# Attention and two feed-forward blocks on one core: a planner that weighs the array's tile form, other ranks, and the opening scores in pieces

## The chip, the core and the metric

One core of a Trainium2 chip. The metric is the device time of one execution in microseconds (us), the median of three runs. Engines: PE is TensorE (matmuls), with PEld for its weight loads, DVE is VectorE, ACT is ScalarE, POOL is GpSimd, SP is the queue that issues all DMAs here. Between engines there are only semaphores, and each engine works off its instructions in the order in which the program was written.

## The reference

Shortened; the inputs are q, k, v of 4 batches, 8 heads, 576 rows and 64 columns, and all sizes are in float32.

```python
# attention: causal window of 128, ALiBi slopes
scores = q @ k.T / 8 + slopes[h] * -abs(i - j)
scores = where((i - j >= 0) & (i - j < 128), scores, -1e9)
attn = exp(scores - max); attn = attn / (sum(attn) + 1e-9)
x = (attn @ v)                     # as 2304 rows of 512
# first block: 512 -> 1024 -> 512
h = x @ w_in
solu = h * softmax(h)
x = (layernorm(solu) * g_ln) @ w_out
# second block: 512 -> 1536 -> 512
out = (silu(x @ w_gate) * (x @ w_val)) @ w_out2
```

## The kernel before

Weights and activations are split into a high and a low fp32r part, so a product of two matrices is three matmuls (lines 605, 938 and 1100). The work runs in three stages that overlap.

**Attention** has 20 steps c (4 batches of 5 steps; the fifth, t = 4, has 64 rows instead of 128) with four pairs of heads each. For each half of a step (two pairs) PE does the *scores* (lines 405 and 412); for each pair DVE, ACT and one of three engines do the softmax (lines 440 to 463), PE transposes the result (line 481), and DVE and ACT copy it to `pt`, once masked (line 488, "late") and once whole (line 491). For each half PE then multiplies with the *values* (line 520): `v` of the step before, and `vd`, the difference of this step's `v` and the last one's.

**First block**: 18 token tiles i. `up(i)` is four pieces of six matmuls of 512 columns (x times w_in, line 605). ACT, DVE and POOL make the solu and the norm, `flip(i)` is eight PE transposes (line 687), and `down1(g)`, for two token tiles, is eight pieces of twelve matmuls of 256 columns (line 605, `lnT` times `wout`).

**Second block**: 36 sets of seven products (line 938). In a set some banks are copied out and written again: s1, s5 and u2 are ACT's copies (lines 954, 959, 961), g1, g2 and v2 are DVE's additions (956, 964, 967), m1 its multiplication (972). The last product, over 252 groups, is line 1100.

All weights come in as 64-bit words and are unpacked ("decode", lines 258 to 266 on ACT, DVE and POOL, then 220 and 224 or 226). Tile `dw` holds what was fetched; `DEC1 = (3, 2)` gives it three buffers while attention runs.

**Tile forms.** Three kinds of matmul use the array in parts: scores with 64 rows by 32 columns (line 412), the scores of a batch's first step with 64 by 128 (line 405), values with 128 by 64, or 64 by 64 for the late products of a short step. Everything else but the transposes of a short step (64 by 128) uses the whole array, 128 by 128.

**The order** is made while the program is written. `Emitter` holds a list of operations that are ready, with a modelled time, and takes, on the engine that is free first, the one with the lowest rank. A rank comes from its task: the step's place for attention (`rank_of`), `i + LEAD` for token tiles, `set_rank` for sets. The modelled cost of a PE operation knows nothing of tile forms.

Of the kernel before, what the change touches and what calls it, by code (L numbers as in the profile page):

```python
# [34 lines left out]
DEC1 = (3, 2)  # L35
# [9 lines left out]
PAIRED = 0  # L45
VDB = 2
PW_2 = -0.5
LEAD = 3.2
R_FLIP = 1.0
R_DOWN = 4.0  # L50
PW_IN = [-0.6, -0.3, -0.29, -0.28, 0.07, 0.08, 0.09, 0.1]
PW_OUT = 4.4
B_DVE = 1600.0
B_ACT = 700.0
HALVES = [(0, 1), (1, 0), (0, 0)]
HB = NC2 // 2


BIAS = {"DVE": B_DVE, "ACT": B_ACT}

# [20 lines left out]

class Emitter:
# [6 lines left out]
    def __init__(self):  # L89
        self.busy, self.pending, self.count, self.open = {}, [], 0, {}  # L90
        self.now = 0.0

# [52 lines left out]
    def _submit(self, at, rank, engine, cost, fn, deps=(), extra=0.0):  # L145
        return self._queue(at, rank, [(engine, cost, fn)], deps, extra)

    def _queue(self, at, rank, ways, deps=(), extra=0.0):
# [3 lines left out]
        op = [rank, self._tick(), at, ways, extra, ev]  # L152
# [12 lines left out]
        return ev  # L165
# [5 lines left out]
    def run(self):  # L171
        while self.pending:
# [7 lines left out]
            t, _, _, op, (engine, cost, fn, *_) = min((x for x in ops if x[0] <= first), key=lambda x: x[1:3])  # L180
# [10 lines left out]
def attention_then_two_ffns(ctx: ExitStack, tc: tile.TileContext, qk, v, w_in, w_out, g_ln, w2, ident_d, base_d, tri_d, out):  # L191
# [58 lines left out]
    def unpack(d, words, got):  # L250

        lw, hw = words[:, :, 0], words[:, :, 1]
        hf = hw.bitcast(F32)
        yield got
        a = lw.bitcast(I32)
        r = yield (ACT, t_act(512), lambda: nc.scalar.activation(a, lw, AF.Copy, scale=2.0 ** -29))  # L258
# [3 lines left out]
        x = yield (ACT, t_act(512), lambda: nc.scalar.activation(bf, hf, AF.Abs, scale=2.0 ** -112))  # L262
        x = yield (DVEP, t_dve(512, True), lambda: nc.vector.tensor_scalar(b, b, 3, None, ALU.logical_shift_left), [x])  # L263
        x = yield (DVEP, t_dve(512), lambda: nc.vector.scalar_tensor_tensor(  # L264
            b, hw, 0x80000000, b, ALU.bitwise_and, ALU.bitwise_or), [x])
        x = yield (POOL, t_pool(512), lambda: nc.gpsimd.tensor_tensor(  # L266
            b.bitcast(I32), b.bitcast(I32), a, ALU.add), [x, r])
        em.give(d["dw"], x)
        return bf, x, d["db"]

    def decode(hi, lo, src, scale=None, even=False):
# [5 lines left out]
        x = yield (high(hi, bf, 512), [x])  # L277
        ways = low(lo, bf, hi, 512)
        x = yield (fair(ways) if even else ways, [x])
# [100 lines left out]
    def score(c, qd):  # L380
# [19 lines left out]
        def scores():  # L400
            for j in range(2):
                if t == 0:
                    for r in range(2):
                        rows = slice(r * D, (r + 1) * D)
                        nc.tensor.matmul(banks[ks[r]][:, j * 256:j * 256 + P], raw[c][rows, 2 * qd + j],  # L405
                                         kt[rows, 2 * qd + j, 0:P], start=True, stop=True)
                    continue
                for i in range(0, n, Q):
                    o, k0 = j * 256 + i, (t - 1) * P + i
                    for r in range(2):  # L410
                        rows = slice(r * D, (r + 1) * D)
                        nc.tensor.matmul(banks[ks[r]][i:i + Q, o:o + P + Q], raw[c][rows, 2 * qd + j, i:i + Q],
                                         kt[rows, 2 * qd + j, k0:k0 + P + Q], start=True, stop=True)

        x = yield (PE, 450 if t == 0 else 450 if t == 4 else 700, scores)
# [9 lines left out]
    def attend(u):  # L425
# [12 lines left out]
        if t:  # L438
# [3 lines left out]
                halves[0:n, :, P:P + n]), [d] + tri_ok)  # L442
        ex, ds, x = [], [], d
        for j in range(2):
            d = yield (DVE, t_dve(P), lambda j=j: nc.vector.tensor_tensor_reduce(  # L445
                e[0:n, j], sc[0:n, j * 256:j * 256 + P], bias[0:n, 2 * pr + j, bs],
                -0.125, 3.0e38, ALU.add, ALU.min, st[0:n, j:j + 1]), [x])
            ds.append(d)
        for j, d in enumerate(ds):
            ex.append((yield (ACT, 93 + t_act(P, True, True), lambda j=j: nc.scalar.activation(  # L450
                e[0:n, j], e[0:n, j], AF.Exp, bias=st[0:n, j:j + 1], scale=-1.0,
                accum_out=sc[0:n, j:j + 1]), [d, ds[0]])))
# [5 lines left out]
        def normalize(eng):  # L458
# [6 lines left out]
        x = yield (DVE, 360, invert, ex)  # L465
# [3 lines left out]
                    (POOL, t_pool(2 * P), lambda: normalize(nc.gpsimd))], [x])  # L469
# [13 lines left out]
        x = yield (PE, 218, flip_p, ident_ok)  # L483
# [3 lines left out]
        if t:  # L487
            ys.append((yield (DVE, t_dve(w), lambda: nc.vector.tensor_tensor(  # L488
                pt[0:n, 1, :, 0:n], tp[0:n, :, 0:n], tri[0:n, 1, 0:n].unsqueeze(1).to_broadcast([n, 2, n]), ALU.mult),
                [x])))  # L490
        ys.append((yield ([(ACT, t_act(w, False), lambda: nc.scalar.copy(pt[:, 0, :, 0:n], tp[:, :, 0:n])),  # L491
                           (DVE, t_dve(w), lambda: nc.vector.tensor_copy(pt[:, 0, :, 0:n], tp[:, :, 0:n]))], [x])))
# [4 lines left out]
        units = (pr - 1, pr) if c >= PAIRED else (pr,)  # L497
        if len(units) == 2 and pr % 2 == 0:
            halved[u].settle(max(y.time for y in ys))
            return  # L500
        if pr < len(units):
            yield px_s
            px_of[c] = yield bank_s
        else:
            yield started[u - len(units)]
        if len(units) == 2:
            yield halved[u - 1]
# [5 lines left out]
        def values():  # L513
            for r in units:
                for late in (1, 0) if t else (0,):
                    kp = n if late else P
                    for j in range(2):
                        h = 2 * r + j
                        src = vd[c] if late else vt[c - 1] if t else vt[c]
                        nc.tensor.matmul(px[j * 64:(j + 1) * 64, r, 0:n], src[0:kp, h * 64:(h + 1) * 64],  # L520
                                         pts[c * NPAIR + r][0:kp, late, j, 0:n], start=(late == 1 or t == 0), stop=(late == 0),
                                         skip_group_check=True)

        x = yield (PE, 100 + 450 * len(units), values, [loaded[c]])
# [15 lines left out]
        while done < n:  # L540
# [7 lines left out]
            y = yield (high(hi, src, 4 * w, False), [x])  # L548
            y = yield (low(lo, src, hi, 4 * w, False), [y])
# [121 lines left out]
    def flip(i):  # L671
# [9 lines left out]
        for q in range(2):  # L681
# [8 lines left out]
            x = yield (PE, 436, turn)  # L690
            y = yield (high(hi, tp, 512, False), [x])
            y = yield (low(lo, tp, hi, 512, False), [y])
# [230 lines left out]
    def products(s):  # L923
# [30 lines left out]
        s1 = yield (ACT, t_act(NH, False), lambda: nc.scalar.copy(t[:, 0], sd), [x1])  # L954
        x6 = yield product(kd, "s2", [x1, s1])
        g1 = yield (DVE, t_dve(NH), lambda: nc.vector.tensor_add(t[:, 0], t[:, 0], sx), [x2, s1])  # L956
        em.give(bank_s, g1, kx)
        g1 = yield (ACT, t_act(NH), lambda: nc.scalar.activation(t[:, 0], t[:, 0], AF.Silu), [g1])  # L958
        s5 = yield (ACT, t_act(NH, False), lambda: nc.scalar.copy(t[:, 2], sb), [x5])  # L959
        x3 = yield product(kb, "s4", [x5, s5])  # L960
        u2 = yield (ACT, t_act(NH, False), lambda: nc.scalar.copy(t[:, 1], sd), [x6])  # L961
        yield y_ok[p][3]
        x7 = yield product(kd, "s3", [x6, u2])
        g2 = yield (DVE, t_dve(NH), lambda: nc.vector.tensor_add(t[:, 1], t[:, 1], sb), [x3, u2])  # L964
        em.give(bank_s, g2, kb)
        g2 = yield (ACT, t_act(NH), lambda: nc.scalar.activation(t[:, 1], t[:, 1], AF.Silu), [g2])
        v2 = yield (DVE, t_dve(NH), lambda: nc.vector.tensor_add(t[:, 2], t[:, 2], sd), [x7, s5])  # L967
# [4 lines left out]
        m1_ = yield (DVE, t_dve(NH), lambda: nc.vector.tensor_mul(t[:, 0], t[:, 0], sd), [x4, g1])  # L972
# [240 lines left out]
```

## Time and profile before

| | us |
|---|---|
| median of three runs (768.16 to 769.06) | 768.61 |
| the profiled execution, its own time | 770.78 |
| its span, first to last instruction | 768.9 |
| PE busy | 736.3 (96%) |
| PEld busy | 667.1 (87%) |
| DVE busy | 556.8 (72%) |
| ACT busy | 452.2 (59%) |
| POOL busy | 227.3 (30%) |

The profile covers one execution. A PE row gives the start of the first matmul of a run and the modelled end of its last; matmuls overlap, so the start of the next row is the better mark for how long a run held the engine. A "granted clock" of 1.0 is TensorE's full rate of 2.4 GHz, 0.5 is 1.2 GHz.

### The profile page before, as it was taken

Reading aid. Unit: us, or ns where it says so; the run is one execution under the profiler, and the core shown is the slowest. Engines: PE = TensorE matmul, PEld = TensorE weight load, DVE = VectorE, ACT = ScalarE, POOL = GpSimd, SP = SyncE. Lnnn points to the kernel's source line nnn. Section 1 sums busy time; section 2 is a strip of 40 time slices with the busy share of each in tenths; the row PEclk is TensorE's granted clock in tenths of the full one; section 3 lists DMA queues with packets and bytes.
Section 4 is the critical chain, followed back from the end, with each engine's and each line's share of the span. In section 5 each row is a group of like instructions: output and inputs, shape, how many; then the busy total and the mean of one; then the engine's idle time right before and its main releaser. Section 6 shows DMA issues by size and latency. Waiting matters only on the chain. (4 is left out here: it accounts for less than half of the span.)

```text
span 768.9 us, 14924 instructions
## 1 busy us (share of the span) xinstructions
PE 736.3 (96%) x5404; PEld 667.1 (87%) x5404; DVE 556.8 (72%) x1522; ACT 452.2 (59%) x1131; POOL 227.3 (30%) x239
## 2 busy tenths in 40 slices
PE   4879999999999999999999999999999999999997
PEld 2547679889887888998999999999999999999997
DVE  5776984674846656779888766877575489896975
ACT  6888985664645556757556655564554474443531
POOL 4667772414232232462013322322221000120200
PEclk9978999999999999999999999999999999999999
DMA  8544421221220101442545554454531599786851
GB/s 276 177 155 118 137 60 46 77 74 46 84 76 14 29 23 45 134 131 64 177 159 189 173 159 170 128 188 145 191 142 45 176 352 329 232 302 194 295 189 64
DMA packets 53641, 110.87 MB, mean 144 GB/s; under 512 B 6464, under 2 KB 23744, under 8 KB 53568
## 3 DMA queue, kind: packets, MB, share of 16 engines
q1 hardware_dynamic: 53568, 109.93, 43.4%
q8 instruction: 42, 0.69, 0.4%
q14 instruction: 31, 0.25, 0.1%
HBM read 80.81 MB, written 29.10 MB: 143 GB/s over the span
## 5 line engine op out<-in xcount | busy, mean ns | idle before, releaser
L938 PE MATMUL bank<-yt,w 128*128 128x384 f32 x1008 | 183.5, 337 | 1.5 <-ACT set L959 1.3
L938 PEld LDWEIGHTS bank<-yt,w 128*128 128x128 f32 x1008 | 175.3, 188 | 3.9 <-ACT set L959 3.1
L1100 PE MATMUL bank<-w,wo 128*128 128x384 f32 x756 | 133.0, 337 | 0.0
L1100 PEld LDWEIGHTS bank<-w,wo 128*128 128x128 f32 x756 | 132.3, 188 | 0.2 <-DVE set L972 0.2
L266 POOL TENSOR_TENSOR db<-db,dw 128x512 int32<-128x512 int32 x52 | 73.5, 1414 | 188.6 <-DVE db L264 142.7
L605 PE MATMUL bank<-lnT,wout 128*128 128x256 f32 x864 | 112.7, 288 | 1.8 <-ACT lnT L220 1.8
L605 PEld LDWEIGHTS bank<-lnT,wout 128*128 128x128 f32 x864 | 107.6, 194 | 5.4 <-ACT lnT L220 2.1
L938 PE MATMUL bank<-shared,w 128*128 128x384 f32 x504 | 95.5, 340 | 2.0 <-ACT set L959 0.8
L938 PEld LDWEIGHTS bank<-shared,w 128*128 128x128 f32 x504 | 87.4, 188 | 6.1 <-DVE set L967 2.8
L605 PE MATMUL bank<-shared,shared 128*128 128x512 f32 x288 | 82.1, 414 | 0.5 <-DVE shared L224 0.5
L450 ACT ACTIVATE e<-e,st 128x128 f32<-128x128 f32 (+1 forms) x160 | 63.2, 401 | 19.0 <-DVE st L445 17.2
L463 POOL TENSOR_TENSOR e<-e,st 128x256 f32<-128x256 f32 (+1 forms) x67 | 42.1, 632 | 79.1 <-DVE st L456 28.0
L605 PEld LDWEIGHTS bank<-shared,shared 128*128 128x128 f32 x288 | 50.7, 191 | 13.4 <-issue 2.6
L220 ACT CAST w<-t 128x768 fp32r<-128x768 f32 (+2 forms) x33 | 26.2, 806 | 41.5 <-DVE t L1054 29.0
L258 ACT ACTIVATE dw<-dw 128x512 int32<-128x512 uint32 x52 | 35.3, 680 | 20.4 <-DMA dw<-w 15.7
L445 DVE CUSTOM_DVE_ANT_0 e<-bank,bias 128x128 f32<-128x128 f32 (+1 forms) x160 | 40.0, 282 | 7.8 <-PE bank L405 4.8
L491 ACT COPY pt<-bank 128x256 f32<-128x256 f32 (+1 forms) x79 | 26.9, 354 | 29.2 <-DVE pt L488 14.1
L481 PE MATMUL bank<-ident,e 128*128 128x128 f32 (+1 forms) x160 | 32.0, 303 | 11.2 <-POOL e L463 8.4
L488 DVE TENSOR_TENSOR pt<-bank,tri 128x256 f32<-128x256 f32 (+1 forms) x64 | 24.0, 385 | 24.9 <-PE bank L481 16.3
L964 DVE TENSOR_TENSOR set<-set,bank 128x384 f32<-128x384 f32 x34 | 18.8, 552 | 31.9 <-PE bank L938 23.0
L220 ACT CAST w<-db 128x512 fp32r<-128x512 f32 (+1 forms) x48 | 27.1, 568 | 21.4 <-POOL db L266 17.8
L481 PEld LDWEIGHTS bank<-ident,e 128*128 128x128 f32 (+1 forms) x160 | 19.4, 154 | 23.2 <-POOL e L463 12.1
(109 smaller groups left out, 1252.6 us busy)
## 6 DMA issues: line engine op xcount, KB each, us to landing
dw<-w SPq DMA_DIRECT2D x36, 512.0 KB, 4.2
t<-ascr SPq DMA_DIRECT2D x21, 768.0 KB, 6.0
ascr<-set SPq DMA_DIRECT2D x34, 384.0 KB, 2.6
later<-ascr SPq DMA_DIRECT2D x15, 768.0 KB, 5.9
wo<-wscr SPq DMA_DIRECT2D x6, 896.0 KB, 7.6
raw<-qk SPq DMA_DIRECT2D x19, 256.0 KB, 2.8
yscr<-ys SPq DMA_DIRECT2D x18, 256.0 KB, 2.2
t<-yscr SPq DMA_DIRECT2D x6, 768.0 KB, 4.9
```

The lines of the kernel that those rows point to most:

```text
L220: return [(ACT, t_act(n, sbuf), lambda: nc.scalar.copy(hi, src)), (DVEP if sbuf else DVE, t_dve(n, sbuf), lambda: nc.vector.tensor_copy(hi ...
L258: r = yield (ACT, t_act(512), lambda: nc.scalar.activation(a, lw, AF.Copy, scale=2.0 ** -29))
L266: x = yield (POOL, t_pool(512), lambda: nc.gpsimd.tensor_tensor(b.bitcast(I32), b.bitcast(I32), a, ALU.add), [x, r])
L445: d = yield (DVE, t_dve(P), lambda j=j: nc.vector.tensor_tensor_reduce(e[0:n, j], sc[0:n, j * 256:j * 256 + P], bias[0:n, 2 * pr + j, bs], ...
L450: ex.append((yield (ACT, 93 + t_act(P, True, True), lambda j=j: nc.scalar.activation(e[0:n, j], e[0:n, j], AF.Exp, bias=st[0:n, j:j + 1], ...
L463: eng.tensor_tensor(e[0:n], e[0:n], st[0:n, 6:8].unsqueeze(2).to_broadcast([n, 2, P]), ALU.mult)
L481: nc.tensor.transpose(tp[:, j, 0:n], e[0:n, j], ident[0:n, 0:n])
L488: ys.append((yield (DVE, t_dve(w), lambda: nc.vector.tensor_tensor(pt[0:n, 1, :, 0:n], tp[0:n, :, 0:n], tri[0:n, 1, 0:n].unsqueeze(1).to_b ...
L491: ys.append((yield ([(ACT, t_act(w, False), lambda: nc.scalar.copy(pt[:, 0, :, 0:n], tp[:, :, 0:n])), (DVE, t_dve(w), lambda: nc.vector.te ...
L605: nc.tensor.matmul(o, terms[m][0], terms[m][1], start=(m == 0), stop=(m == len(terms) - 1))
L938: nc.tensor.matmul(o, l, r, start=first and m == 0, stop=m == 5, skip_group_check=True)
L1100: nc.tensor.matmul(o, w[:, b], ob[k, i][a][:, j], start=i == 0 and m == 0, stop=i == HB - 1 and m == 2)
```

## The change

The planner gets three rules for PE that hold once its modelled time is past 100 us (`TOGETHER`, in ns). Scores carry form 1 and values form 2, all else form 0. From form 0 it does not begin scores or values while fewer than three such operations (`LEAST`) are ready and none of them has been ready for 540 ns (`PATIENCE`). Once in a form it stays with operations of that form, then of any form above 0. A change of form adds 95 ns to the modelled cost.

Besides: an offset to the rank of single operations (`O_...`; the largest are -1.3 for the flips of a token tile, -1.2 for g1, g2 and m1 of a set and for the copies of transposed softmax, +0.3 for x and +0.5 for scores); other ranks for w_in and w_out, `LEAD`, `R_FLIP`, `PW_2`, another bias against DVE; a fourth `dw` buffer and a third `vd` buffer. The scores of a batch's first step are cut into the 32-column pieces of the other steps (16 matmuls of 128 columns instead of 4). In a short step the late products of both pairs come before the others, and only the first pair's matmul carries `start`. The number of instructions of each kind on DVE, ACT and POOL stays the same but for a few that move between these engines.

```diff
-DEC1 = (3, 2)
+DEC1 = (4, 2)
-VDB = 2
-LEAD = 3.2
-R_FLIP = 1.0
+VDB = 3
+LEAD = 3.373
+R_FLIP = 0.751
-PW_IN = [-0.6, -0.3, -0.29, -0.28, 0.07, 0.08, 0.09, 0.1]
+PW_IN = [-0.6, -0.23, -0.29, -0.28, 0.25, 0.26, 0.43, 0.28]
+O_FLIP = -1.299
+O_FREE = -1.226
+TOGETHER = 100000.0
+PATIENCE = 540.469
+LEAST = 3
...
-            t, _, _, op, (engine, cost, fn, *_) = min((x for x in ops if x[0] <= first), key=lambda x: x[1:3])
+            ops = [x for x in ops if x[0] <= first]
+            if ops[0][4][0] == "PE" and first > TOGETHER:
+                tiled = [x for x in ops if form(x)]
+                if 0 < len(tiled) < len(ops) and not self.form:
+                    if len(tiled) < LEAST and min(x[3][2] for x in tiled) > first - PATIENCE:
+                        ops = [x for x in ops if not form(x)]
+                elif tiled and self.form:
+                    same = [x for x in tiled if form(x) == self.form]
+                    ops = same or tiled
+            t, _, _, op, (engine, cost, fn, *_) = min(ops, key=lambda x: x[1:3])
+            if engine == "PE":
+                if first > TOGETHER and getattr(fn, "form", 0) != self.form:
+                    cost += 95.0
+                self.form = getattr(fn, "form", 0)
...
-                if t == 0:
+                for i in range(0, n, Q):
+                    o, k0, w = (j * 256, 0, P) if t == 0 else (j * 256 + i, (t - 1) * P + i, P + Q)
...
+                        nc.tensor.matmul(banks[ks[r]][i:i + Q, o:o + w], raw[c][rows, 2 * qd + j, i:i + Q],
+                                         kt[rows, 2 * qd + j, k0:k0 + w], start=True, stop=True)
...
+            todo = [(r, late) for r in units for late in ((1, 0) if t else (0,))]
+            if t == 4:
+                todo.sort(key=lambda x: -x[1])
```

What moves is shown at three places. The lines of the changed kernel are others: 441, 553, 511, 721, 639 and 972 are its scores, values, transposes of softmax, flips, up and down pieces, and products of sets; 255 is its copy to a high part, 293 and 297 decode, 988, 992, 993 and 995 are s1, the silu, s5 and u2.

PE in the middle of attention, in the third group of two token tiles (`lnT` and `wout` are a down piece, `pt` with `vd` or `v` values). Before:

```order
L481 MATMUL bank_80<-ident,e 128x128 x2
L605 MATMUL bank_85<-lnT_2074,wout_76 128x256 x8
L605 MATMUL bank_85<-lnT_2075,wout_75 128x256 x4
L520 MATMUL bank_80<-pt,vd 64x128 x2
L520 MATMUL bank_80<-pt,v 64x128 x2
L520 MATMUL bank_80<-pt,vd 64x128 x2
L520 MATMUL bank_80<-pt,v 64x128 x2
L605 MATMUL bank_85<-lnT_2075,wout_75 128x256 x4
L605 MATMUL bank_85<-lnT_2074,wout_75 128x256 x8
L481 MATMUL bank_87<-ident,e 128x128 x2
L605 MATMUL bank_84<-lnT_2074,wout_76 128x256 x8
L605 MATMUL bank_84<-lnT_2075,wout_75 128x256 x4
```

and in the changed kernel, at the values of the same half step:

```order
L639 MATMUL bank_86<-lnT_2172,wout_76 128x256 x8
L639 MATMUL bank_86<-lnT_2173,wout_75 128x256 x8
L639 MATMUL bank_86<-lnT_2172,wout_75 128x256 x8
L553 MATMUL bank_87<-pt,vd 64x128 x2
L553 MATMUL bank_87<-pt,v 64x128 x2
L553 MATMUL bank_87<-pt,vd 64x128 x2
L553 MATMUL bank_87<-pt,v 64x128 x2
L441 MATMUL bank_84<-keys,raw 32x160
L441 MATMUL bank_83<-keys,raw 32x160
```

Where pieces, transposes and values took turns, the values now come behind two pieces together (24 matmuls), and scores (16 rows, the first two are shown) follow them without a whole-array matmul between.

PE in the opening: the second half of the first token tile's up pieces (`shared` holds x and w_in). Before, these follow the third transpose of step 5 (`ident`, `e`):

```order
L481 MATMUL bank_86<-ident,e 128x128 x2
L481 MATMUL bank_82<-ident,e 128x128 x2
L605 MATMUL bank_86<-shared_74,shared_73 128x512 x4
L605 MATMUL bank_86<-shared_73,shared_74 128x512 x4
L605 MATMUL bank_86<-shared_73 128x512 x4
L481 MATMUL bank_84<-ident,e 128x128 x2
L605 MATMUL bank_85<-shared_74,shared_73 128x512 x4
L605 MATMUL bank_85<-shared_73,shared_74 128x512 x4
L605 MATMUL bank_85<-shared_73 128x512 x4
```

In the changed kernel they come with step 3's last transpose, and that step's second half of values stands between them:

```order
L511 MATMUL bank_82<-ident,e 128x128 x2
L639 MATMUL bank_80<-shared_74,shared_73 128x512 x4
L639 MATMUL bank_80<-shared_73,shared_74 128x512 x2
L553 MATMUL bank_86<-pt,vd 64x128 x2
L553 MATMUL bank_86<-pt,v 64x128 x2
L553 MATMUL bank_86<-pt,vd 64x128 x2
L553 MATMUL bank_86<-pt,v 64x128 x2
L639 MATMUL bank_80<-shared_73,shared_74 128x512 x2
L639 MATMUL bank_80<-shared_73 128x512 x4
```

So transposes and values of step 4 now stand among the up pieces of the first two token tiles, and all of step 5 behind them.

PE where the first block ends (`yt` and `w` are a product of a set, `lnT` and `wout` the last group's down pieces, `e_4173` and `e_4278` the last token tile's normed values, to be flipped). Before:

```order
L687 MATMUL bank_85<-ident,e_4173 128x128 x4
L938 MATMUL bank_81<-yt_0_3945,w_3948 128x384 x2
L938 MATMUL bank_81<-yt_0_3946,w_3947 128x384 x2
L938 MATMUL bank_81<-yt_0_3945,w_3947 128x384 x2
L605 MATMUL bank_87<-lnT_4324,wout_76 128x256 x8
L605 MATMUL bank_87<-lnT_4325,wout_75 128x256 x8
L605 MATMUL bank_87<-lnT_4324,wout_75 128x256 x8
L605 MATMUL bank_87<-lnT_4324,wout_76 128x256 x8
L605 MATMUL bank_87<-lnT_4325,wout_75 128x256 x8
L605 MATMUL bank_87<-lnT_4324,wout_75 128x256 x8
L938 MATMUL bank_80<-yt_0_3945,w_3948 128x384 x2
L938 MATMUL bank_80<-yt_0_3946,w_3947 128x384 x2
```

In the changed kernel:

```order
L721 MATMUL bank_84<-ident,e_4278 128x128 x4
L972 MATMUL bank_82<-yt_0_4007,w_4010 128x384 x2
L972 MATMUL bank_82<-yt_0_4008,w_4009 128x384 x2
L972 MATMUL bank_82<-yt_0_4007,w_4009 128x384 x2
L972 MATMUL bank_81<-yt_0_4007,w_4010 128x384 x2
L972 MATMUL bank_81<-yt_0_4008,w_4009 128x384 x2
L972 MATMUL bank_81<-yt_0_4007,w_4009 128x384 x2
L972 MATMUL bank_82<-yt_0_4007,w_4010 128x384 x2
L972 MATMUL bank_82<-yt_0_4008,w_4009 128x384 x2
L972 MATMUL bank_82<-yt_0_4007,w_4009 128x384 x2
L639 MATMUL bank_85<-lnT_4429,wout_76 128x256 x8
L639 MATMUL bank_85<-lnT_4430,wout_75 128x256 x8
```

Two more products of the first set (the one that needs s5, and the one that needs u2) moved ahead of the last group's down pieces.

ACT at the same place, from s1 on. Before (s5 is the eighteenth instruction from here):

```order
L954 COPY t_4309<-bank_81 128x384
L220 CAST lnT_4324<-bank_84 128x4x128
L220 CAST lnT_4324<-bank_86 128x4x128
L220 CAST w_3951<-db 128x256
L258 ACTIVATE dw<-dw 128x512
L262 ACTIVATE db<-dw 128x512
L220 CAST shared_73<-t_4308 128x384
L220 CAST shared_73<-t_4308 128x2x384
L220 CAST lnT_4324<-bank_82 128x4x128
L220 CAST lnT_4324<-bank_85 128x4x128
L220 CAST w_3951<-db 128x512
```

In the changed kernel:

```order
L988 COPY t_4394<-bank_82 128x384
L255 CAST lnT_4429<-bank_86 128x4x128
L255 CAST lnT_4429<-bank_87 128x4x128
L255 CAST w_4013<-db 128x256
L293 ACTIVATE dw<-dw 128x512
L297 ACTIVATE db<-dw 128x512
L992 ACT_TABLE_LOAD
L992 ACTIVATE t_4394<-t_4394 128x384
L255 CAST lnT_4429<-bank_83 128x4x128
L255 CAST lnT_4429<-bank_84 128x4x128
L993 COPY t_4394<-bank_81 128x384
L995 COPY t_4394<-bank_82 128x384
```

Between s1 and s5 stood sixteen instructions and now stand nine. The casts of the last token tile's flips are the eighth and ninth after s1 in both, with the silu and its table load ahead of them now and behind them before.

## Rows read from the trace of the kernel before

**Rows 1.** Busy time by stretch: length; PE, PEld, DVE, ACT, POOL; clock, DMA.

```profile
31.00:48.20 17.20, 11.54 (x160) 7.60 (x160) 14.76 (x72) 14.95 (x53) 12.16 (x12) 1.00 0.55 177
48.20:65.20 17.00, 16.50 (x135) 11.22 (x136) 11.04 (x61) 12.84 (x50) 9.81 (x12) 0.50 0.53 157
65.20:112.40 47.20, 44.89 (x403) 33.32 (x401) 39.96 (x147) 43.55 (x126) 35.35 (x37) 1.00 0.27 87
112.40:342.60 230.20, 228.88 (x2137) 195.20 (x2130) 146.66 (x588) 137.26 (x434) 81.02 (x105) 1.00 0.21 62
342.60:366.80 24.20, 22.45 (x156) 21.99 (x155) 20.03 (x36) 15.51 (x28) 7.47 (x5) 0.93 0.36 120
366.80:634.00 267.20, 263.66 (x1485) 257.19 (x1484) 197.65 (x356) 151.93 (x293) 52.79 (x44) 1.00 0.50 170
```

**Rows 2.** What PE waited for, 0 to 100 us: total, times, longest.

```profile
PE bank L481 <- POOL e L463: 8.2, 6, 1.8
```

**Rows 3.** Order of time on PE, 176 to 215 us: start, length, engine, line.

```profile
186.21 4.58 PE L605 MATMUL bank<-lnT,wout 128*128 128x256 f32 x36
190.72 0.78 PE L412 MATMUL bank<-keys,raw 64*32 64x160 f32 x32
191.42 1.09 PE L687 MATMUL bank<-ident,e 128*128 128x128 f32 x8
...
201.93 0.75 PE L412 MATMUL bank<-keys,raw 64*32 64x160 f32 x16
202.60 1.70 PE L605 MATMUL bank<-lnT,wout 128*128 128x256 f32 x12
...
212.62 0.33 PE L520 MATMUL bank<-pt,vd 64*64 64x64 f32 x4
...
213.67 0.46 PE L481 MATMUL bank<-ident,e 64*128 64x64 f32 x4
```

**Rows 4.** The same view, 100 to 125 us.

```profile
110.68 0.44 PE L520 MATMUL bank<-pt,vd 128*64 128x128 f32 x4
...
111.71 0.77 PE L412 MATMUL bank<-keys,raw 64*32 64x160 f32 x32
112.41 1.66 PE L605 MATMUL bank<-shared,shared 128*128 128x512 f32 x6
```

**Rows 5.** The same view, 225 to 262 us.

```profile
227.07 0.72 PE L405 MATMUL bank<-keys,raw 64*128 64x128 f32 x8
227.71 1.66 PE L605 MATMUL bank<-shared,shared 128*128 128x512 f32 x6
...
236.56 1.34 PE L412 MATMUL bank<-keys,raw 64*32 64x160 f32 x64
237.83 6.01 PE L605 MATMUL bank<-lnT,wout 128*128 128x256 f32 x48
```

**Rows 6.** The same view, 329 to 400 us.

```profile
331.05 11.67 PE L605 MATMUL bank<-lnT,wout 128*128 128x256 f32 x96
342.56 1.22 PE L938 MATMUL bank<-yt,w 128*128 128x384 f32 x6
...
347.40 1.29 PE L938 MATMUL bank<-yt,w 128*128 128x384 f32 x6
350.44 7.67 PE L605 MATMUL bank<-lnT,wout 128*128 128x256 f32 x48 [1.75 <-ACT lnT L220]
```

**Rows 7.** Order of time on ACT, 343 to 357 us.

```profile
345.88 0.48 ACT L954 COPY t<-bank 128x384 f32<-128x384 f32 x1
...
349.77 1.10 ACT L220 CAST lnT<-bank 128x512 fp32r<-128x512 f32 x2
...
353.59 1.28 ACT L958 ACT_TABLE_LOAD   x1
...
355.31 0.46 ACT L959 COPY t<-bank 128x384 f32<-128x384 f32 x1
```

**Rows 8.** What PE's weight loads waited for, 340 to 625 us.

```profile
PEld bank L938 <- ACT set L959: 5.0, 8, 1.2
```

More of the change, by code (lines that the diff above doesn't have):

```diff
@@ L56 @@
 HB = NC2 // 2
+O_MAX = 0.0
+O_EXP = -0.005
+O_INV = 0.0
+O_TURN = 0.136
+O_PT = -1.188
+O_VAL = 0.0
+O_X = 0.316
+O_SC = 0.496
+O_DEC = 0.0
+O_SPL = -0.05
+O_FLIP = -1.299
+O_LN = 0.0
+O_SET = 0.0
+O_FREE = -1.226
+TOGETHER = 100000.0
+PATIENCE = 540.469
+LEAST = 3
 BIAS = {"DVE": B_DVE, "ACT": B_ACT}
@@ L79, in __init__, with form @@
         self.free, self.queue = [(0.0, i) for i in range(n)], []
+def form(entry):
+    return getattr(entry[4][2], "form", 0)
 class Emitter:
@@ L91, in __init__ @@
         self.now = 0.0
+        self.form = 0
     def start(self, gen, rank):
@@ L401, in scores @@
             for j in range(2):
-                if t == 0:
+                for i in range(0, n, Q):
+                    o, k0, w = (j * 256, 0, P) if t == 0 else (j * 256 + i, (t - 1) * P + i, P + Q)
                     for r in range(2):
                         rows = slice(r * D, (r + 1) * D)
[L405 to L415, printed above, removed]
+                        nc.tensor.matmul(banks[ks[r]][i:i + Q, o:o + w], raw[c][rows, 2 * qd + j, i:i + Q],
+                                         kt[rows, 2 * qd + j, k0:k0 + w], start=True, stop=True)
+        scores.form = 1
+        x = yield (PE, 450 if t == 0 else 450 if t == 4 else 700, scores, (), 0.0, O_SC)
         yield x
@@ L496, in attend @@
         pts[u] = pt
-        units = (pr - 1, pr) if c >= PAIRED else (pr,)
-        if len(units) == 2 and pr % 2 == 0:
+        size = NPAIR if c >= WHOLE else 2
+        if pr % size < size - 1:
             halved[u].settle(max(y.time for y in ys))
             return
-        if pr < len(units):
+        units = range(pr + 1 - size, pr + 1)
+        if pr < size:
             yield px_s
@@ L504, in attend @@
         else:
-            yield started[u - len(units)]
-        if len(units) == 2:
-            yield halved[u - 1]
+            yield started[u - size]
+        for r in units[:-1]:
+            yield halved[c * NPAIR + r]
         px = banks[px_of[c]].rearrange("p (r q) -> p r q", r=NPAIR)
@@ L513, in values @@
         def values():
[L514 to L524, printed above, removed]
+            todo = [(r, late) for r in units for late in ((1, 0) if t else (0,))]
+            if t == 4:
+                todo.sort(key=lambda x: -x[1])
+            for r, late in todo:
+                kp = n if late else P
+                for j in range(2):
+                    h = 2 * r + j
+                    src = vd[c] if late else vt[c - 1] if t else vt[c]
+                    nc.tensor.matmul(px[j * 64:(j + 1) * 64, r, 0:n], src[0:kp, h * 64:(h + 1) * 64],
+                                     pts[c * NPAIR + r][0:kp, late, j, 0:n], start=r == 0 and (late == 1 or t == 0), stop=(late == 0),
+                                     skip_group_check=True)
+        values.form = 2
+        x = yield (PE, 100 + 450 * len(units), values, [loaded[c]], 0.0, O_VAL)
         for r in units:
```

70 lines of the change are left out of this document (35 added, 35 removed).

## The prediction

> **What bounds the kernel now.** I read the busy time by stretch first [rows 1]. From 112.4 us on, where the seventh token tile's up pieces begin, PE is the bound: busy 228.88 of 230.20 us to the end of the first block, 263.66 of 267.20 in the sets of products. Here only fewer or cheaper PE pieces count. Before 112.4 us it is otherwise. PE is busy 11.54 of 17.20 us, 16.50 of 17.00 and 44.89 of 47.20, while ACT is busy 14.95, 12.84 and 43.55: decode and softmax share ACT, and PE waits for the softmax, 8.2 us for POOL's part alone [rows 2]. The granted clock is 0.50 (1.2 GHz) from 48.2 to 65.2 us, after a stretch in which PE had gaps, and 1.00 around it; PE is full there because everything takes twice as long.
>
> Then I read PE in order of time for what a form costs. Thirty-six down matmuls begin at 186.21 and the scores after them at 190.72 [rows 3]: 4.51 us. Undisturbed, 96 of them take 342.56 - 331.05 = 11.51 us, 0.120 each [rows 6], so 36 should take 4.32. The 0.19 left over is what one trip out of the whole-array form costs beside the trip's own pieces: about half where the run begins behind a form change, half where it hands over. The scores hold PE from 190.72 to 191.42, 0.70 us [rows 3], also when values stand ahead of them: 111.71 to 112.41 [rows 4], with the values at 110.68 to 111.71, 1.03. So values and scores in a row make one trip of two.
>
> **The change part by part.**
>
> *Fewer trips.* I counted PE's order between the seventh token tile's first up piece and the first product of a set. It has 45 trips before and 27 after; form changes fall from 115 to 84. Eighteen trips less at 0.19 are **-3.4 us**. All of it is on the path, as PE is the bound in this stretch. From both sides: -1.7 if handing over alone is saved, -4.1 if an up piece (twice the columns) pays 0.23.
>
> *Bunched transposes.* They too are followed by a slow first matmul, half of the 0.19; 26 returns from transposes to pieces instead of 33: **-0.6**, bounds -0.7 and 0.
>
> *Short steps.* Late products first makes two inner changes fewer in each of 6 groups here. Such a group takes 212.62 to 213.67, 1.05 us [rows 3], as long as a full one [rows 4] with half the columns, so its four changes do cost. At 0.05 a change: **-0.6**; bounds 0 and -1.2 (at 0.1).
>
> *Opening scores in pieces.* One group takes 0.64 us now (227.07 to 227.71) [rows 5]. In pieces it looks like the 160-column scores, 0.70, by columns 0.56. Four groups here: between +0.3 and -0.3; I take **-0.2**, since number seems to cost little: a short step's scores, with half as many matmuls of the same width, hold PE for 0.67 (201.93 to 202.60) [rows 3]. Two scores in a row also share their end, 1.27 us (236.56 to 237.83) instead of 1.41 [rows 5]; one more such pair, **-0.1**.
>
> The Trainium skill, page "TensorEngine Tiling (Array Packing)", section "Instruction Overhead", speaks against this edit: each matmul carries some 60 cycles whatever its width. By it 32 matmuls of a group would take an estimated 0.8 us at full clock, and all eight groups would lose 1.3 us together. The 0.67 and 0.70 us for 16 and 32 matmuls disagree.
>
> Together **-4.9 us**.
>
> *New waits in this stretch.* PE is idle 1.3 us of it now. The shortest distance in PE work from scores to their transposes is 3.8 us after and 3.9 before; from transposes to values 1.2 after (one place, step 8) and 1.6 before; before, places as near as these showed no wait to speak of. But scores that follow values, and steps that begin in bunches, put more softmax on DVE and ACT at once. I take **-0.3**, bounds -1.3 and +3.
>
> *End of the first block.* Now PE waits 1.75 us for the last cast of the flips, 350.44 [rows 6]; nothing waits for s5, which ends at 355.77, 9.9 us after s1 began [rows 7], as its product stands behind half of the last down pieces. In the new order this product stands ahead of them. ACT has nine instructions between s1 and s5: four casts at the 0.55 us of [rows 7], one shorter, two of decode, the table load of 1.28, the silu, some 5.6 us in all. s5 ends 6.5 us after 345.88, at 352.4. PE would be there about a microsecond after 347.40, one product later, at 348.5, and waits 3.9, with the flips' casts then done. 3.9 instead of 1.75 would be +2.1; as ACT's casts may come a little earlier with one flip's wait gone, I take **+1.5**, bounds -1 and +3. The clock's dip there (0.93 in the mean [rows 1]) I leave as it is.
>
> *Sets of products.* From the fourth set on ACT's and DVE's orders are the old ones but for a few neighbours; the earlier g1 has no row that it would shorten for PE except the 5.0 us for s5 [rows 8], behind the silu that waits for g1. **0**, bounds -1.5 and +1.5.
>
> *The opening.* The work ahead of 112.4 us is the same: 68.6 us of PE pieces in both orders, 219 ACT instructions instead of 217, 361 on DVE instead of 364. What differs is what is late. The second half of the first token tile comes with step 3, not step 5, so step 5's scores stand behind 32 us of PE pieces instead of 21, and w_in's last part must be there earlier (the fourth `dw` buffer and the ranks serve that: its last cast is ACT's 104th instruction instead of the 125th). I take **+0.5**: with the clock at half again, PE has about as much behind it at 65 us. Bounds -5 and +6 are the rivals below.
>
> Sum: -4.9 - 0.3 + 1.5 + 0 + 0.5 = -3.2 us on a span of 768.9; the profiled execution's 770.78 is 1.9 more than its span and 2.2 over the median. Carried to the median: 768.6 - 3.2 = **765.4 us**.
>
> **Rivals.**
>
> *The opening gets slower* (ends above 768.6). The six up pieces from the first tile's second half to the second tile's end now stand where the clock was at 0.50 [rows 1]. Each is six matmuls of twice the columns of a down matmul, 6 x 0.24 = 1.4 us at full clock by [rows 6]; at half six cost 8.2 us more. ACT meanwhile lacks step 5, whose scores are behind them; it has 2 us or so of decode in hand. Then 6 us more than forecast: 771.4. It decides if the clock is at half again and step 5's scores begin after some 72 us. For it: PE's gaps ahead of 48 us remain. Against it: up pieces need no softmax, and attention's own pieces were just as slow there. 17 in 100.
>
> *The opening gets faster.* Early up pieces fill PE's gaps, ACT's idle time from 31 to 65 us (17.20 - 14.95 + 17.00 - 12.84 = 6.4 us) shrinks, or the clock stays up. At most 6.4, I take 5: 760.4. 16 in 100.
>
> *Gathering is paid back in waits.* Operations held back for a bunch start their chains later; 27 trips with 0.15 us of wait each, and bank or slot waits as the one of 2 us at 350, give 3 to 4 back: 769. Against it: the distances above. 17 in 100.
>
> **How the numbers follow.** The forecast has 50 in 100; its own range, 762.5 to 768, comes from the bounds of the middle and the block's end. The range for 8 in 10 takes in most of both openings: 759.5 to 771. A measurement tells 0.2%, 1.5 us, from no change: faster is below 767.1, slower above 770.1. From forecast, faster opening and gathering, faster: 0.46 + 0.16 + 0.02 = 0.64; from forecast, gathering and slower opening, same: 0.04 + 0.13 + 0.02 = 0.19; from slower opening and gathering, slower: 0.15 + 0.02 = 0.17.
>
> **What would show it.** The stretch from the seventh token tile's up pieces to the first product should fall from 230.2 to about 225, with scores and values as adjacent rows of unchanged 0.70 and 1.03 us, and opening scores of 0.56 to 0.70. The seventh tile should begin at 112.9, within 106 and 119. A wait of about 4 us for s5 should stand ahead of the last down pieces and none at them. The sets should keep their waits. It is wrong if trips fall but the stretch doesn't, or if the opening moves by more than the middle.

## The result

The changed kernel takes 759.88 us (median of 4 runs, 759.56 to 760.32), the kernel before 768.50 beside it (4 runs): a ratio of 0.9887, 95% interval 0.987 to 0.9905, or 8.6 us less. The forecast was 765.4, 3.2 us less; its range of 759.5 to 771.0 holds the time, its lower end only just. Direction and place were right, the size was not.

Stage by stage, with marks in PE's order of time: the seventh token tile's first up piece, the first product of a set, the first product of the second set, the first of the last product's groups. The first two columns of times are the first profiles of both kernels, the next two a second pair, profiled on one chip (runs e5 and e6 below).

| stage, us | before | after | before, e5 | after, e6 | forecast | measured in the second pair |
|---|---|---|---|---|---|---|
| opening | 112.41 | 110.69 | 110.99 | 109.88 | +0.5 | -1.1 |
| middle | 230.15 | 223.39 | 230.36 | 223.39 | -5.2 | -7.0 |
| end of the first block | 24.28 | 22.19 | 22.38 | 22.19 | +1.5 | -0.2 |
| sets of products | 258.61 | 257.78 | 259.44 | 259.71 | 0 | +0.3 |
| last product | 143.47 | 143.74 | 143.68 | 143.94 | no term | +0.3 |

### The profile page after: what moved, and what is told of

Its sections match the earlier page's. It is cut to its first block, busy times and chain, and to the rows that moved or that the text cites. A ratio compares the mean times of both kernels' runs of the same rounds, so it can differ in the third digit from the quotient of the medians.

```text
span 757.8 us, 15332 instructions
## 1 busy us (share of the span) xinstructions
PE 724.2 (96%) x5596; PEld 660.9 (87%) x5596; DVE 554.2 (73%) x1517; ACT 455.6 (60%) x1142; POOL 223.9 (30%) x237
## 5 line engine op out<-in xcount | busy, mean ns | idle before, releaser
L301 POOL TENSOR_TENSOR db<-db,dw 128x512 int32<-128x512 int32 x52 | 71.5, 1376 | 190.7 <-DVE db L299 130.8
L639 PE MATMUL bank<-lnT,wout 128*128 128x256 f32 x864 | 109.1, 284 | 0.0
L639 PEld LDWEIGHTS bank<-lnT,wout 128*128 128x128 f32 x864 | 105.8, 191 | 1.9 <-issue 0.8
L493 POOL TENSOR_TENSOR e<-e,st 128x256 f32<-128x256 f32 (+1 forms) x63 | 38.9, 623 | 69.9 <-DVE st L486 30.3
L441 PE MATMUL bank<-keys,raw 64*32 64x160 f32 (+1 forms) x1152 | 32.7, 322 | 9.3 <-DMA keys<-qk 9.3
L511 PE MATMUL bank<-ident,e 128*128 128x128 f32 (+1 forms) x160 | 30.2, 292 | 11.2 <-POOL e L493 4.3
L639 PE MATMUL bank<-shared 128*128 128x512 f32 x144 | 38.8, 391 | 0.0
```

The lines of the kernel that those rows point to most:

```text
L441: nc.tensor.matmul(banks[ks[r]][i:i + Q, o:o + w], raw[c][rows, 2 * qd + j, i:i + Q], kt[rows, 2 * qd + j, k0:k0 + w], start=True, stop=True)
L511: nc.tensor.transpose(tp[:, j, 0:n], e[0:n, j], ident[0:n, 0:n])
L639: nc.tensor.matmul(o, terms[m][0], terms[m][1], start=(m == 0), stop=(m == len(terms) - 1))
```

## The profile after

Busy time by stretch of the changed kernel, the answer to [rows 1] (length; PE, PEld, DVE, ACT, POOL; clock, DMA):

```profile
31.00:48.20 17.20, 13.89 (x186) 8.91 (x170) 13.94 (x58) 14.66 (x50) 10.58 (x11) 1.00 0.51 157
48.20:65.20 17.00, 15.24 (x106) 10.88 (x107) 11.99 (x54) 13.90 (x45) 9.98 (x11) 0.80 0.43 138
65.20:110.69 45.49, 41.65 (x481) 30.35 (x479) 39.43 (x167) 42.23 (x133) 34.13 (x38) 1.00 0.28 87
110.69:334.08 223.39, 222.42 (x2233) 194.51 (x2225) 150.38 (x592) 140.10 (x444) 77.67 (x101) 1.00 0.22 70
334.08:356.26 22.18, 20.86 (x156) 20.48 (x155) 18.04 (x32) 13.77 (x25) 7.93 (x7) 1.00 0.25 74
356.26:634.00 277.74, 274.99 (x1551) 268.18 (x1550) 206.29 (x370) 160.94 (x306) 54.15 (x45) 1.00 0.52 178
```

In the middle PE does the same work in 222.42 us instead of 228.88, and its idle time goes from 1.32 to 0.97: the gain is cheaper work, not fewer waits. PE in order of time where gathered work stands (start, length, engine, line):

```profile
201.15 1.69 PE L639 MATMUL bank<-lnT,wout 128*128 128x256 f32 x12
202.77 0.45 PE L553 MATMUL bank<-pt,vd 64*64 64x64 f32 x8
203.15 0.45 PE L553 MATMUL bank<-pt,v 128*64 128x64 f32 x8
203.53 0.67 PE L441 MATMUL bank<-keys,raw 64*32 64x128 f32 x32
204.13 0.45 PE L553 MATMUL bank<-pt,vd 64*64 64x64 f32 x8
204.50 0.45 PE L553 MATMUL bank<-pt,v 128*64 128x64 f32 x8
204.89 4.58 PE L639 MATMUL bank<-lnT,wout 128*128 128x256 f32 x36
209.31 2.00 PE L639 MATMUL bank<-shared,shared 128*128 128x512 f32 x8
```

Three groups make one trip out of the whole-array form. A short step's values take 203.53 - 202.77 = 0.76 us, against 1.05 in [rows 3]; opening scores in pieces 0.60, against 0.64 in [rows 5]. The 36 down matmuls behind the trip, which hand over to pieces of their own form, take 4.42 us: 4.32 and 0.10 for the return. In [rows 3] the same 36 took 4.51, with values ahead of them and scores behind.

The end of the first block, PE and then ACT (in brackets idle time and what ended it):

```profile
334.08 1.22 PE L972 MATMUL bank<-yt,w 128*128 128x384 f32 x6
...
338.91 1.29 PE L972 MATMUL bank<-yt,w 128*128 128x384 f32 x6
341.52 2.36 PE L972 MATMUL bank<-yt,w 128*128 128x384 f32 x12 [1.31 <-ACT t L993]
343.72 5.91 PE L639 MATMUL bank<-lnT,wout 128*128 128x256 f32 x48
```

```profile
334.32 0.59 ACT L255 COPY ys<-bank 128x512 f32<-128x512 f32 x1 [2.00 <-PE bank L639]
335.33 0.48 ACT L988 COPY t<-bank 128x384 f32<-128x384 f32 x1 [0.42 <-PE bank L972]
...
338.31 1.28 ACT L992 ACT_TABLE_LOAD   x1
...
340.97 0.49 ACT L993 COPY t<-bank 128x384 f32<-128x384 f32 x1
```

The wait for s5 stands where it was forecast, ahead of the last down pieces, and none at them ([rows 6] had 1.75 there); it is 1.31 us, not 3.9.

## Experiments

The runs were made four at a time, each four on another chip, and the sets of products took up to 5.5 us more in one kernel than in another with the same order of PE there (last section). So verdicts go by stages of the profiles first.

**One local edit undone.**

```diff
-            if t == 4:
-                todo.sort(key=lambda x: -x[1])
```

> The changed kernel with the short steps' products in the old order (late, whole, late, whole); PE's order of groups stays as it is. Theory A (from the changed kernel's rows: a short step's two late and two whole groups take 0.76 us now, 1.05 before): each of 8 groups takes 0.29 us more, 6 of them in the middle, so the middle grows from 223.4 to 225.2 us and the whole kernel by 2.3 to 762.2. Theory B (the forecast's 0.05 per inner change): 0.10 per group, 0.8 us in all, 760.7; the rest of the 0.29 came from elsewhere.

Measured: 763.59 us (ratio to before 0.9932, 0.9917 to 0.9947). The order of PE's groups is that of the changed kernel, and the middle takes 225.15, 1.76 more: theory A. A group of values takes 204.04 - 202.98 = 1.06 again:

```profile
202.98 0.33 PE L551 MATMUL bank<-pt,vd 64*64 64x64 f32 x4
203.24 0.34 PE L551 MATMUL bank<-pt,v 128*64 128x64 f32 x4
203.51 0.33 PE L551 MATMUL bank<-pt,vd 64*64 64x64 f32 x4
203.77 0.34 PE L551 MATMUL bank<-pt,v 128*64 128x64 f32 x4
204.04 0.67 PE L441 MATMUL bank<-keys,raw 64*32 64x128 f32 x32
```

So two changes inside values cost 0.29, 0.15 each. It is the change of form and not the taking of turns: a full step's values take turns in the same way within one form, and take 1.03 us with twice the columns ([rows 4]).

**Both local edits alone, in the kernel before.** Nothing else is changed.

```diff
-                if t == 0:
+                for i in range(0, n, Q):
+                    o, k0, w = (j * 256, 0, P) if t == 0 else (j * 256 + i, (t - 1) * P + i, P + Q)
...
+            if t == 4:
+                todo.sort(key=lambda x: -x[1])
```

> The kernel before with only the two local edits: opening scores in 32-column pieces, and a short step's late products first. The order of the groups stays that of before. Theory A: opening scores 0.60 instead of 0.645 us in 8 groups (-0.4), short steps 0.76 instead of 1.05 in 8 groups (-2.3), so 2.0 of it in the middle (230.2 to 228.2) and 765.8 in all. Theory B (forecast): short steps -0.8, scores -0.4, 767.3. As its opening is that of before, about 17 us at half clock should stay. The dip of the clock behind the last flips' wait stays if it belongs to that order, and is gone if the profiled execution of before was an odd one (its time was 2.2 us above its median).

Measured: the middle takes 228.20, 1.95 less than the first profile of before, as theory A says; short steps make 1.76 of it and opening scores 0.24. The whole kernel takes 768.12 (ratio 0.9989, 0.9976 to 1.0002), less gain than either theory: in its profile the sets took 261.98 us, 2.5 more than in e5 with the same order, so a gain ahead of the sets can drown in what they vary by. The low clock at the block's end is absent; the one of the opening lasts 20.5 us.

**The rules for tile forms taken out of the change.**

```diff
-TOGETHER = 100000.0
+TOGETHER = 1.0e12
```

> The changed kernel without the planner's rules for tile forms (the threshold set beyond the end); all ranks, buffers and local edits stay. 43 trips out of the whole-array form in the middle instead of 27, 101 form changes instead of 84. Theory A (the trips carry the gain): the middle grows by 16 x 0.19 = 3.0 us and some tenths for transposes, to about 226.7, and the opening, which is the same up to 100 us of planned time, stays at 110.7; in all about 763.1. Theory B (the ranks carry it): the middle stays within 1 us of 223.4 and the time within 1 us of 759.9.

Measured: 770.09 (ratio 1.0015, 1.0003 to 1.0027), slower than before. The middle takes 228.40, 5.0 more than with the rules, and 0.2 more than e2, which has the old ranks: without the rules the new ranks are worth nothing in the middle. Theory B falls; theory A's 3.0 was too low (PE is busy 4.0 us longer and idle 1.0). That the whole kernel is slower than before, though its middle is not, lies behind the middle: in its profile the sets took 263.25 us, 3.5 more than in e6 with the same order of PE.

**The rules alone, in the kernel before.**

```diff
+        scores.form = 1
...
+        values.form = 2
...
+                if 0 < len(tiled) < len(ops) and not self.form:
...
+                    cost += 95.0
```

> The kernel before with only the planner's rules for tile forms; ranks, buffers and local code as before. 25 trips in the middle instead of 45, 92 form changes instead of 115. Theory A: 20 x 0.19 = 3.8 us and some tenths for transposes off the middle, 230.2 to about 226; the opening stays at 112.4 with 17 us at half clock, the end of the first block may move by 2 either way; 764.5 in all. Theory B (gathering is paid back in waits unless the new ranks go with it): the middle keeps 229 or more, with waits of PE for softmax of some 3 us, and 768.

Measured: 764.87 (0.9952, 0.9939 to 0.9965). The middle takes 227.88, only 2.3 less. The up and down pieces fall as far as they should, from 168.83 to 164.15 us (each row from its start to that of the next), but PE is idle 2.96 us instead of 1.32. Waits of PE there (total, times, longest):

```profile
PE bank L505 <- POOL e L487: 1.0, 2, 0.6
PE bank L428 <- DVE lnT L247: 0.7, 1, 0.7
PE bank L505 <- DVE lnT L247: 0.6, 1, 0.6
PE bank L505 <- DVE pt L512: 0.5, 1, 0.5
```

Lines 505 and 428 are transposes and scores here. Both theories are half right: with the old ranks, gathering is paid back in part.

**Both kernels again, on one chip.** No edit.

> The kernel before, unchanged, profiled anew beside the changed kernel. Theory A (PE's order sets the middle, the clock's low stretches fall where an execution lets them): the middle is 230.2 us again within 0.2; the low clock of 3.4 us behind the last flips' wait, which cost 1.7 us in the first profile, is absent, so the end of the first block (first product of a set to first product of the second) takes about 22.4 instead of 24.3; the opening differs by up to 1.7 us from 112.4 without any change of order. Theory B (the low clock belongs to this order): 24.3 again.

> The changed kernel, unchanged, profiled anew on the same chip. Theory A: middle 223.4, end of the first block 22.2, both within 0.2; against the kernel before on this chip the opening and the sets differ by less than 1 us each, so that the middle's 6.8 carries nearly the whole difference of 8 to 9. Theory B (the opening and the clock carry 2 us or more of it): the opening is shorter by 2 or more again.

Measured: before 768.71, after 760.35 (0.9886, 0.9866 to 0.9905), profiled executions 768.70 and 760.90. The stretches of the second pair, before and then after:

```profile
110.99:341.35 230.36, 228.81 (x2136) 195.15 (x2129) 148.42 (x588) 137.26 (x434) 80.97 (x105) 1.00 0.21 63
341.35:363.73 22.38, 21.12 (x157) 20.61 (x156) 19.84 (x36) 15.13 (x28) 7.37 (x5) 1.00 0.33 106
363.73:623.17 259.44, 254.95 (x1436) 248.51 (x1436) 190.04 (x345) 145.31 (x284) 52.81 (x44) 1.00 0.49 165
```

```profile
109.88:333.27 223.39, 222.44 (x2232) 194.51 (x2225) 149.45 (x592) 139.88 (x444) 77.49 (x101) 1.00 0.23 69
333.27:355.47 22.20, 20.89 (x157) 20.50 (x155) 18.73 (x33) 13.76 (x25) 7.88 (x7) 1.00 0.27 82
355.47:615.18 259.71, 255.14 (x1436) 248.24 (x1435) 188.08 (x341) 146.32 (x285) 53.97 (x45) 1.00 0.48 163
```

The middle repeats within 0.2 us and carries 7.0 of the 7.7 by which these two spans differ. The block's end takes 22.38 in e5, 1.9 less than in the first profile of the same order: the 48 down matmuls behind the flips' wait take 6.09 us without the low clock instead of 7.51, and the wait is 1.26 instead of 1.75. The low clock went with one execution, not with the order, and is part of why that first profiled execution, 770.78, was 2.2 above its median.

**All offsets of single operations at zero.**

```diff
-O_PT = -1.188
+O_PT = 0.0
...
-O_FLIP = -1.299
+O_FLIP = 0.0
...
-O_FREE = -1.226
+O_FREE = 0.0
```

> The changed kernel with all rank offsets of single operations at zero; the rules for tile forms, the other ranks, the buffers and the local edits stay. 23 trips in the middle instead of 27, 80 form changes instead of 84. Theory A (the offsets keep the softmax ahead of PE, and without them gathering is half paid back in waits, as in the kernel before with the rules alone): 4 x 0.2 = 0.8 less for trips and some 2 us of waits more, the middle about 224.6. Theory B (the offsets do nothing for PE): 222.6, and a faster kernel.

Measured: 760.98 (0.9907, 0.9882 to 0.9933), not to be told from the changed kernel; the middle 223.71, between the theories. PE is idle 2.05 us in it instead of 0.97 and busy 221.66 instead of 222.42: the offsets keep some 1.1 us of waits off, half of what theory A expected, and cost most of that again in trips.

**The old ranks with everything else of the change.**

```diff
-PW_2 = -0.766
-LEAD = 3.373
-R_FLIP = 0.751
+PW_2 = -0.5
+LEAD = 3.2
+R_FLIP = 1.0
...
-PW_OUT = 5.23
-B_DVE = 1876.064
+PW_OUT = 4.4
+B_DVE = 1600.0
```

> The changed kernel with the old ranks of w_in, w_out and token tiles and the old bias against DVE; offsets, buffers, rules and local edits stay. 50 trips in the whole program instead of 55. Its opening is another (the seventh token tile begins earlier in the work), so the time from the start to the first product of a set counts: 334.1 in the changed kernel. Theory A (the ranks only shift the opening): 334 within 2. Theory B (the ranks keep the waits off): 336 or more, with waits of PE for the softmax of 2 us more than now.

Measured: 770.67 (1.0018, 1.0004 to 1.0033). The first product comes at 343.06, 9 to 10 us later than in the changed kernel: theory B's time, and more than it said, but not its cause. PE's waits from 50 to 136.8 us, in e8 (the two longest rows):

```profile
PE bank L553 <- DVE shared L259: 3.0, 1, 3.0
PE bank L511 <- POOL wout L261: 1.7, 1, 1.7
```

and the stretches there, first of e8, then of the changed kernel (e6):

```profile
50.00:90.00 40.00, 35.06 (x328) 25.65 (x320) 31.01 (x127) 35.74 (x108) 27.86 (x29) 0.91 0.40 127
90.00:136.80 46.80, 41.88 (x445) 34.32 (x445) 31.78 (x141) 34.06 (x116) 21.93 (x27) 0.93 0.24 71
```

```profile
50.00:90.00 40.00, 39.26 (x359) 28.63 (x366) 32.38 (x135) 37.39 (x118) 28.30 (x32) 0.94 0.43 134
90.00:136.80 46.80, 43.17 (x499) 34.78 (x497) 34.79 (x155) 35.17 (x116) 24.79 (x29) 1.00 0.22 66
```

PE is idle 9.9 us in e8, 4.4 in e6; these 5.5 are the larger part of the 9.8 between the two, and PE's busy time up to the first product is 3.3 longer. The longest waits of transposes and values on PE are not for the softmax but for DVE's and POOL's work on x, w_in and w_out.

**The rules and both local edits, old ranks and buffers, no offsets.** The kernel before with the edits of e2 and e4 together.

```diff
+            if t == 4:
+                todo.sort(key=lambda x: -x[1])
...
+        values.form = 2
```

> The kernel before with the rules for tile forms and both local edits; ranks, offsets and buffers are those of before. 25 trips in the middle, 81 form changes. Theory A (the parts add, and without the new ranks gathering loses some 2.4 us to waits): the middle is 227.9 - 2.0 = 225.9, against 223.4 in the changed kernel; the end of the block 22.2; in all about 763. Theory B (the waits in the rules-only kernel were chance of that one order): 223.5 to 224.5.

Measured: 763.16 (0.9929, 0.9908 to 0.9951); the middle 226.24, with PE idle 3.1 us: theory A.

**The same with the new buffers.**

```diff
-DEC1 = (3, 2)
+DEC1 = (4, 2)
...
-VDB = 2
+VDB = 3
```

> The kernel of e9 with the fourth fetch buffer and the third buffer for the difference of v as well: all of the change but ranks and offsets. The planner now starts the seventh token tile later in PE's order (row 758 instead of 608), as with the old ranks in e8. Time from the start to the first product of a set counts. Theory A (more fetch buffers let decode run ahead of softmax, and the old ranks let it, so the opening loses as in e8): 342 or more. Theory B (it was the offsets that spoiled e8's opening): 336 to 338, like e9.

Measured: 764.24 (0.9944, 0.9923 to 0.9964); first product at 337.46, against 337.26 in e9: theory B. The buffers are worth nothing by themselves and don't spoil the opening; in e8 it was the offsets together with the old ranks, as with new ranks and no offsets (e7) the first product comes at 334.12.

**Only `LEAD` and `R_FLIP` back.**

> The changed kernel with only LEAD and R_FLIP back at their old values (3.2 and 1.0). 27 trips in the middle as before this edit, 82 form changes instead of 84. Theory A (how far token tiles trail attention keeps the softmax ahead of PE): the middle grows by 1.5 us or more, to 225 or above, with waits for the softmax that the changed kernel hasn't. Theory B (the ranks of the weights do it): 223.4 within 0.5.

Measured: 764.30 (0.9945, 0.9928 to 0.9962). The middle takes 225.29 with PE idle 2.06 us, and the opening 112.28: theory A. These two numbers, by which token tiles trail attention, give 1.9 us of the middle, 1.1 of it PE's idle time.

**Waiting longer for company.**

```diff
-PATIENCE = 540.469
-LEAST = 3
+PATIENCE = 3000.0
+LEAST = 6
```

> The changed kernel with a planner that waits longer for company: LEAST 6 instead of 3, PATIENCE 3000 instead of 540 ns. 25 trips in the middle instead of 27, 80 form changes instead of 84. Theory A (trips at 0.2 us each, no new waits): the middle 223.0, the kernel at 759.9, not to be told from the changed one. Theory B (waiting longer brings waits): 224 or more. A faster kernel by over 1 us is expected by neither.

Measured: 769.72 (1.0009, 0.999 to 1.0028). Two trips less, and the middle takes 227.77, 4.4 more: theory B. Not all of this is lost: a flip of 0.8 us now stands ahead of the first product, and the end of the first block, without a wait for s5, takes 19.80 instead of 22.19. Up to the second set 2.0 us remain. The stretch and PE's largest waits in it:

```profile
110.88:338.65 227.77, 223.96 (x2240) 195.82 (x2233) 147.31 (x586) 135.38 (x434) 79.09 (x103) 1.00 0.21 63
```

```profile
PE bank L511 <- ACT pt L521: 1.4, 2, 0.7
PE bank L511 <- DVE st L485: 1.0, 1, 1.0
PE bank L511 <- DVE mst L670: 0.5, 1, 0.5
```

PE is idle 3.8 us, and its busy time is 1.5 longer, 0.8 of it the flip. Most of what the whole kernel loses lies behind: the sets, which have another order here, take 265.97 us, 6 to 8 more than in the changed kernel. No variant beats the changed kernel.

## Why the prediction was right, and where it was wrong

The place and the mechanism of the gain were right, and its size was less than half of what was measured. The second pair differs by 4.5 us more than the forecast 3.2: 1.8 us of this lie in the middle (1.2 of them the short steps), 1.7 at the end of the first block and 1.6 in the opening; sets and last product take 0.6 back.

**Trips, transposes and waits in the middle: right.** Forecast -3.4 - 0.6 - 0.3 = -4.3. Up and down pieces went from 168.83 to 163.37 us, flips and transposes from 23.29 to 23.92, together -4.8. A fit over the runs of up and down pieces in the profiles gives 0.13 (up) or 0.10 (down) for a return from scores or values, 0.09 to 0.11 for handing over to them, and 0.08 to 0.10 behind transposes. By it the counted changes fall by some 3.7 us, from 9.4 to 5.7, against the forecast 4.0. Of what else the pieces fell by, 0.9 is what PE waited behind them in the kernel before and no longer does; some 0.8 the fit leaves open. The flips and transposes take 0.6 more, 0.4 of it waits.

**Short steps: mis-sized by three.** Forecast -0.6, at 0.05 per inner change, bounded at -1.2. Measured -1.76 (e1, e2), 0.15 per change and outside the bounds. I had noted that such a group takes as long as a full one with half the columns and drew no price from it. The trace of before had the right neighbour: opening values, eight matmuls of 128 columns in one form, with as many columns in all (end of this section). They take 233.99 - 233.40 = 0.59; 1.05 less 0.59 over three inner changes is 0.15.

**Opening scores: right.** -0.24 in the middle against -0.2. The Trainium skill, page "TensorEngine Tiling (Array Packing)", section "Instruction Overhead", with its 60 cycles for each matmul, is not borne out here: the group took 0.60 us with 32 matmuls, 0.64 with 8.

**End of the first block: wrong, +1.5 against -0.2.** The step that failed took s1's start of 345.88 from [rows 7] as a fixed distance from its product. It wasn't: s1 stood behind a copy to `ys` that waited 3.89 us for the transfer that empties `ys`' only buffer. ACT in the kernel before, first profile:

```profile
345.39 0.59 ACT L220 COPY ys<-bank 128x512 f32<-128x512 f32 x1 [3.89 <-DMA yscr<-ys]
345.88 0.48 ACT L954 COPY t<-bank 128x384 f32<-128x384 f32 x1
```

That transfer stood on SP behind fetches of weights that waited for their buffers:

```profile
331.22 9.47 SPq L212 DMA_DIRECT2D dw<-w  x3
340.79 0.38 SPq L212 DMA_DIRECT2D yscr<-ys  x1
```

It went out 1.3 us after the copy whose result it carries had ended (339.50), and then took 4.5 us to land, the longest of such transfers from 300 to 360 us:

```profile
DMA to landing us min/median/max: 2.1/2.3/4.5
```

The landing counts for more than the late start. In e2 the transfer began 0.15 us after its copy, but again right behind a fetch; it landed after 4.3 us, and ACT stood 3.77 us. In e5 it landed after 4.6, and ACT stood 3.97. In the changed kernel the transfer begins right after its copy, ahead of the next fetch and 3.4 us ahead of the set's first product:

```profile
330.68 0.38 SPq L247 DMA_DIRECT2D yscr<-ys  x1
```

It lands after 2.3 us, and no such transfer from 295 to 345 us takes longer:

```profile
DMA to landing us min/median/max: 2.1/2.1/2.3
```

So s1 starts 1.25 us behind that product's start (335.33 - 334.08), not 3.32 (345.88 - 342.56). The path from s1 to the end of s5 was forecast well, 6.13 us against 6.5. So PE waits 1.31, about as long as it waited for the flips in e5 (1.26), and the stage stays as it was. In the first pair the low clock, which I left "as it is", adds 1.4, and a longer wait for the flips 0.5.

**Sets: not contradicted.** 0 forecast, +0.3 in the second pair, -0.8 in the first; by what the sets vary by (last section) an effect of a microsecond would not show.

**Opening: wrong in sign, within its bounds.** +0.5 forecast, -1.7 and -1.1 measured. Executions of before's opening order took 110.77 (e4), 110.99 (e5) and 112.41, of the changed one 109.83 (e3), 109.88 (e6), 110.31 (e1), 110.69 and 110.88 (e12): about 1 us is the change's. The forecast took the work ahead of the seventh tile as the same and put nothing here for the local edits, though two short-step groups and four groups of opening scores lie in the opening. With these edits and the old ranks it took 110.03 (e2) and 111.02 (e9), so how much of the 1 us the order brings is not shown. Both opening rivals fall, and with them the price that they put on the clock: with 17.1 us at half clock (e6) the changed opening ended earlier than with 6.8 us. (At [rows 6]'s 0.24 us a matmul, the first rival's six pieces would cost 8.6 us more at half clock, not 8.2.) That the opening can move by 9 us showed in e8; there the cause is a mixture of offsets and ranks, and which offset it is stays open.

**The rival on gathering: its mechanism is real.** It was to pay 3 to 4 us back. With old ranks it takes 1.6 to 1.8 (idle time 2.96 and 3.1 in e4 and e9 against 1.32), with more patience 2.8 (e12 against the changed kernel's 0.97). The changed kernel escapes it by its ranks: half of this idle time comes back when only `LEAD` and `R_FLIP` go (2.06, e11), as much when only the offsets go (2.05, e7). Neither had a term of its own in the forecast. By the runs the 7.0 us come apart as 2.0 for the local edits (e1, e2), 2.3 for the rules (e4) and some 2.8 for ranks, offsets and buffers (223.39 against e9's 226.24), which give nothing without the rules (e3).

The row that would have priced the short steps, from the trace of before:

```profile
233.40 0.66 PE L520 MATMUL bank<-pt,v 128*64 128x128 f32 x8
233.99 0.66 PE L481 MATMUL bank<-ident,e 128*128 128x128 f32 x4
```

## What to carry to other kernels

To price a change of tile form, set a group with such changes beside one of as many columns without. An instruction's start in the old trace is no constant: look at what released it and the one ahead of it on its engine before a sum is built on it. Short stores that free a buffer are better issued ahead of long fetches on the same queue; here they landed in 2.3 us instead of 4.5. Gathering work by form shortened PE's work in every kernel that had it, but with the old ranks about 1.7 us of it went into waits; ranks that begin the chains behind that work earlier kept these off. Waiting longer for company cost more here than the two trips that it saved.

## What the runs showed of the hardware

The low clock (0.5) of the opening lay elsewhere in each execution, for 17.1 (first profile, without the block's end) to 23.9 us (e5) in before's order and 6.8 to 17.1 us in the changed one, and hardly moved the opening's end; in these two orders all of it lay in the first 65.2 us, where PE had gaps. In the sets the changed kernel itself differed by 1.9 us between its two profiles (257.78 and 259.71), and kernels with the same order of PE there by more: 260.57 in e1 and 263.25 in e3, and with before's order from 257.55 in e4 to 261.98 in e2. One place where it arises: a fetch of weights landed late, ACT's copies for the set stood behind it, and PE waited for them. In e1, ACT and then PE (ACT's next copies come behind this instruction):

```profile
455.72 0.66 ACT L293 ACTIVATE dw<-dw 128x512 int32<-128x512 uint32 x1 [2.20 <-DMA dw<-w]
```

```profile
457.34 1.31 PE L970 MATMUL bank<-shared,w 128*128 128x384 f32 x6 [1.39 <-ACT set L993]
```

In the changed kernel's first profile ACT waited 0.79 us for this fetch, and PE hardly at all. What makes a fetch land late stays open.
